# Attention and a feed-forward layer in one kernel: half of the small loads on GpSimd's queue, two pairs of token blocks merged, and a new written-out order

## The chip, the core and the metric

The kernel runs on one core of one Trainium2 chip. The metric is the device time of one execution in microseconds (us). The core has TensorE for matrix multiplication (PE in the profile; its weight loads are PEld), VectorE (DVE), ScalarE (ACT), GpSimd (POOL) and SyncE (SP), which here only issues transfers and transposes by DMA. Each engine works through its own instructions strictly in the order in which the program lists them.

## What is computed

The input is q, k and v for 4 batches, 12 heads, 448 tokens and 64 columns per head, all float32, and two weight matrices.

```python
scores = q @ k.T / sqrt(64)                    # causal: masked above the diagonal
attn = exp(scores - max) / (sum + 1e-9)
x = (attn @ v) as (4 * 448 tokens, 768)        # heads side by side
h = x @ w_in                                   # 768 -> 2048
g = h * sigmoid(1.702 * h)
out = g @ w_out                                # 2048 -> 768, (1792, 768) float32
```

## The kernel before

**Chunks and blocks.** The 1,792 tokens are 28 chunks of 64. `TUNE["groups"]` cuts them into nine blocks, each a run of chunks of one batch: block 0 is chunks 0 to 3 of batch 0, block 1 chunks 0 to 2 of batch 1, blocks 2 and 3 are chunks 0 to 3 and 4 to 6 of batch 2, blocks 4 and 5 the same of batch 3, blocks 6 and 7 chunks 3 to 4 and 5 to 6 of batch 1, and block 8 chunks 4 to 6 of batch 0. A block's width for TensorE is 64 columns for each of its chunks: 256, 192, 256, 192, 256, 192, 128, 128 and 192.

**Attention of a block** runs over six units u of two heads. Blocks 0 and 1 compute in float32 and turn q and k on TensorE (`load_heads`, `turn`, `k_unit32`, `q_unit32`; lines 888 to 953). From block 2 on, every float32 operand is split into two float16 parts, and k and q come in pairs of units: `k_pair` (from line 955) loads k for units u and u+1 with four transfers (line 965: units a = 0, 1, heads j = 0, 1 of each) into the one buffer `kk`, finds its scale, splits it and turns it with a DMA transpose (line 990); `q_pair` (from line 997) does the same for q with four transfers (line 1010) into the one buffer `qq`, copies each part once more (line 1053 on GpSimd or 1051 on VectorE), and `q_unit` turns it (line 1068). Then come the scores (1090 in float32, 1099 in float16), the mask and row maximum (1122), the exponential (1136), the row sums' small instructions (1256, 1262), the split of the probabilities, a DMA transpose of them (1283), and the product with v (1302), whose result for two units is written as two float16 parts into `xT`.

**The weights.** `w_in` and `w_out` come in as raw words and are put into another form by ScalarE and VectorE (`to_f32`, lines 541 to 592), summed for their scale (`gram`, line 616) and split in two float16 parts (`split`). A slice of `w_out` is loaded raw into a borrowed buffer that `TUNE["raw"]` names: W for the weights' own room, K for `kk`, V for `vraw`, P for the probabilities.

**The feed-forward layer of a block.** `moe(n)` calls `h_slice` for eight slices of 256 columns of w_in: 72 matmuls of the block's width for each slice (line 410, in four groups of 18; each instruction works on a 64-column half, and the two halves stand next to each other in the order), then tanh on ScalarE (1401) and the product on VectorE (1406), and the result is split into `gT`. `out_tile` (two chunks at a time) multiplies `gT` with w_out: 8 groups of 12 matmuls of 384 columns (line 1442) for each half of the output, one scaling instruction (468) and the store (1468). `xT` and `gT` are rings with places for seven chunks.

**The order.** Every step is registered with `add`: which engines could do it, what it reads and writes. The program is not emitted in the order of registration but in that of the string `ORDER`: a number is the step, the letter the engine (S for SP, P for TensorE, A, D, and G for GpSimd). The list before has 2,968 steps: 806 of TensorE, 1,033 of VectorE, 645 of ScalarE, 335 of SP and 149 of GpSimd. All transfers are S. The numbers in the braces of an `add` call are the planner's costs with which such an order was made; they put nothing into the program.

Of the kernel before, what the change touches and what calls it, by code (L numbers as in the profile page):

```python
# [9 lines left out]
F32 = mybir.dt.float32  # L10
# [16 lines left out]
    raw=(['W11', 'K0', 'V0', 'P0', 'W13', 'W15', 'K0', 'P0'], ['W11', 'W13', 'W15', 'V0', 'K0', 'P0', 'V0', 'P0']),  # L27
# [22 lines left out]
    wi2=2.63,  # L50
    parts=(((0, 1), (1, 3), (3, 6)), ((0, 3), (3, 6))),
# [3 lines left out]
1D 3G 2A 60S 0G 4S 45S 57S 9S 541G 14S 108S 61P 49S 5A 62A 6D 7A 84P 27S 8D 47S 58P 85A 59A 111S 10D 82P 491S 11A  # L55
46S 70P 12A 83D 13D 15A 159S 63P 71D 162S 73D 16A 109P 64D 447S 66D 74A 17D 93P 444S 72A 110D 65A 18D 86P 67A 75P
77D 96D 19P 28A 78D 94D 32S 87D 133P 89D 97A 20D 29D 79P 48S 95A 76D 21P 68P 88A 112P 22D 90A 30D 80A 98P 24D 100D
23D 113A 31D 134A 432S 121P 69A 101D 25A 99D 135P 122D 114P 124D 50S 91P 136D 123A 160P 115D 117D 125A 144P 26D 118A
436S 116A 137P 161A 163P 92A 102P 145D 164A 215S 147D 184P 146A 140D 210S 128D 148A 186P 138D 494S 129D 185D 141A
119P 103D 434S 172P 33A 187D 165P 139A 34D 81P 538S 173D 35A 168D 126P 166D 433S 175D 188P 169A 151D 120D 195P 167A  # L60
36D 174A 437S 51P 176A 191D 189D 152D 127A 196D 104P 198D 192A 52D 37P 190A 179D 228S 105D 197A 573S 53P 130P 216D
199A 545S 448P 54D 38D 217A 180D 202D 445P 56D 55D 131D 39P 149P 617D 40D 449D 106A 153P 218D 446A 42D 469P 107D
211A 142P 203D 450P 219D 150A 233S 467P 143A 435S 132P 212D 154A 470A 451D 155P 43A 213D 453D 170P 214D 177P 468A
457P 156D 452A 181P 251S 171A 41D 44D 178A 471P 193P 157A 200P 182A 454A 495P 458D 229A 204P 158D 246S 478P 194A
472D 492P 474D 459A 230D 183P 201A 479D 220P 205A 462D 231D 496A 493A 626D 324S 206P 463D 473A 232D 480A 497P 475A
504P 207D 552A 514P 221D 455P 500D 234A 498D 222P 483D 516P 505D 264S 484D 438P 223D 515A 456D 208A 235D 460P 225D
517A 439D 618P 236D 226A 209D 518P 336S 237D 440P 619P 461A 252A 224D 227D 238P 499A 501A 464P 247A 269S 525P 620P
253D 465A 635D 506A 521D 254D 476P 522A 248D 621P 553A 255D 477A 330S 325A 627P 239D 249D 622A 441D 481P 519D 250D
520A 240P 539P 482A 628P 265A 287S 443D 509D 526D 510D 241D 623D 527A 574P 629P 540A 266D 624A 243D 242D 530D 267D
244A 256P 282S 625D 630P 268D 575A 337A 485P 257D 245D 466P 631A 258P 576P 300S 487P 270A 636P 632D 486A 271A 259D  # L70
577D 502P 261D 644D 488D 637P 633A 544S 579D 272D 262A 593P 634D 638P 273D 503A 645P 288A 263D 305S 578A 639P 594A
489A 260D 274P 580A 289D 640A 531D 490D 507P 283A 646P 275D 641D 508A 290D 276P 331A 595P 284D 511P 291D 647P 301A
285D 642A 583P 277D 512A 302D 648P 596A 326A 286D 523P 643D 597P 649A 292P 279D 524A 303D 551A 654P 327D 280A 293D
304D 294P 528P 513P 295D 328D 306A 655P 297D 281D 529A 354S 298A 532P 534P 656P 307D 533A 550A 299D 581P 308A 657P
582A 338A 309D 318S 332A 278D 584D 310P 339D 585A 650D 604P 333A 311D 586P 340D 312P 651A 313D 598D 587A 588D 360S
600D 355A 315D 589D 535D 590P 652D 316A 653D 605D 663P 662D 334D 599A 601A 317D 393S 591A 319A 602P 658A 664P 320D
606A 342S 659D 603A 348S 536A 321D 607P 356A 665P 609D 296D 537D 777S 322D 660A 592P 361A 666P 661D 375S 608A 357D
362A 323P 610D 672P 671D 314D 358D 667A 611P 363D 394A 399S 673P 668D 612A 442D 680D 364D 613P 669A 674P 343A 670D
# [12 lines left out]
1031A 1346D 770G 709D 894S 772A 926D 733P 797D 1032D 928G 710D 864G 811A 746P 1193S 798A 927G 800A 773D 809A 734P
711A 1194S 812D 1039A 747P 799D 774S 712D 1033A 735P 1195A 801D 817D 713A 810D 748P 819D 845S 830D 930A 828D 736P
818A 714D 844S 932G 820A 829A 749P 842S 931D 821G 831A 843S 722D 715A 1034D 737P 933G 822D 1040D 1073S 1196A 832G
1052D 750P 716D 823A 1192S 825A 1200A 833D 824D 738P 826D 836A 1076S 1349D 1347D 1361D 751A 834D 837D 717A 881P 813S
835D 1053P 1362D 1041D 1199A 718D 846A 870P 1054P 1075S 882D 1202A 884D 739P 838S 719A 873D 871D 1042D 883A 906P
720D 885A 895P 847P 1055P 1074S 874A 848D 886G 872A 850D 849D 740P 959S 1201A 851D 929G 1198A 875G 887D 1056P 852D
1197A 741A 934S 814P 888A 876D 1203D 890D 1047A 753P 877D 889D 879A 891D 853S 1077A 1057P 907D 909D 908A 878D 754P
880D 910A 896D 1078D 898D 897A 911G 1058P 742S 1048D 899A 1080G 1079D 892S 1049A 1081D 900G 912D 755P 915A 913D
1050D 1082A 1204P 839P 901D 916D 904A 1209S 1084G 756P 914D 902A 1083D 840A 1208S 905D 1059P 1085G 903D 841D 1211S
757P 1205D 917S 1207D 1206G 946P 935P 1929D 758P 1994D 947D 938D 1086S 948A 936D 1060P 949D 939A 2540D 937A 950A  # L100
759P 1210S 940D 941D 951D 942A 944D 960P 752S 952D 971P 945D 953A 760P 943D 1132S 955A 963D 954D 964A 1108S 918P
961D 956D 761A 893P 972D 962A 1087P 974D 1063P 973A 965G 1995D 957S 975A 2553D 919A 1088P 966D 1061D 976G 1064P
# [102 lines left out]
class Ops:  # L205
# [16 lines left out]
    @staticmethod  # L222
    def turned(tiles):

        return {"SP": max(1.6, 0.2 * tiles - 0.65)}
# [66 lines left out]
def kernel(  # L292
# [74 lines left out]
    ps_o, ps_o_r = bufs(2, [P, 512], F32, "ps_o", pp)  # L367
    ps_t = ps_o[0]
    XC = 448
    ps_x_r = Ring(2)  # L370

    w_in32 = w_in.bitcast(I32)
    w_out32 = w_out.bitcast(I32)
# [1194 lines left out]
```

## Time and profile before

| | |
|---|---|
| median of 3 runs | 582.08 us (581.81 to 583.6) |
| the profiled execution's own time | 581.97 us |
| its span, first to last instruction | 580.3 us, 24,080 instructions |
| TensorE (PE) busy | 564.2 us, 97% of the span |
| its weight loads (PEld) busy | 475.5 us, 82% |
| VectorE busy | 424.6 us, 73% |
| ScalarE busy | 365.2 us, 63% |
| GpSimd busy | 60.8 us, 10% |
| granted TensorE clock | 1.000 over the whole span (full speed, 2.4 GHz) |
| chain that ended last | PE 78%, DVE 12%, DMA 4%, ACT 2%, issue 1% |

A span is the time from the first to the last instruction; what the execution's own time has over it lies before and after. Busy time is the union of an engine's instructions. A matmul's own duration is longer than the step from one matmul to the next, since they are pipelined; the steady cost of a group is read where the same group repeats without a gap.

### The profile page before, as it was taken

To read this page: it belongs to the slowest core of one execution; us is meant where nothing else is said; L and a number is where in the kernel's file an instruction comes from. 1 tells how busy PE (TensorE), PEld (TensorE's weight loads), DVE (VectorE), ACT (ScalarE), POOL (GpSimd) and SP (SyncE) were. 2 spreads that over 40 slices of the span, in tenths; PEclk is the share of its full clock that TensorE was granted. 3 is DMA by queue.
4 is the path that set the end of the run, shared out by engine and by line. 5 is a ranking of instruction groups with operands and counts; after the bars stand their busy time and mean duration, and the time that the engine had idled before them with its cause. 6 is when DMAs were issued, how large, how long until landed. Compare 5 with 4: busy or idle time off the path is not lost.

```text
span 580.3 us, 24080 instructions
## 1 busy us (share of the span) xinstructions
PE 564.2 (97%) x10376; PEld 475.5 (82%) x10376; DVE 424.6 (73%) x1201; ACT 365.2 (63%) x879; POOL 60.8 (10%) x165
## 2 busy tenths in 40 slices
PE   6999979999999999999999999999999999999997
PEld 4778868988788998779977899778987978889965
DVE  3899999999998688778758759555887987823110
ACT  5899999899976566458746556364665555512210
POOL 2000000013120102101100103011102020000000
PEclk9999999999999999999999999999999999999999
DMA  8999659588997968899846967877758957620010
GB/s 267 268 275 371 199 165 334 180 190 161 187 194 152 155 124 155 141 164 170 155 71 130 154 122 111 130 157 132 119 110 141 139 97 113 107 61 3 16 28 28
DMA packets 228187, 86.70 MB, mean 149 GB/s; under 512 B 208880, under 2 KB 217840, under 8 KB 228080
## 3 DMA queue, kind: packets, MB, share of 16 engines
q1 hardware_dynamic: 228080, 85.16, 72.4%
q8 instruction: 81, 1.33, 1.0%
q14 instruction: 26, 0.21, 0.1%
HBM read 44.63 MB, written 5.51 MB: 86 GB/s over the span
## 4 chain that ended last, share of the span: by engine, by line
PE 78%; DVE 12%; DMA 4%; ACT 2%; issue 1%; SPq 1%; DVEq 0%; ACTq 0%
PE ps_o L1442 33%; PE ps_h L410 30%; PE ps_v L1302 5%; PE ps_s L1099 5%; DVE wob L592 2%; DVE wob L473 2%; PE ps_s L1090 2%; PE ps_o L913 2%; DMA wob<-in_moe_w_out_dram 2%; DMA gT<-in_k_dram 1%; PE ps_h L903 1%; DVE ps_h L1406 1%; DVE wob L558 1%; DMA out_dram<-ob 1%; DVE wob L577 1%
## 5 line engine op out<-in xcount | busy, mean ns | idle before, releaser
L410 PE MATMUL ps_h<-xT,wib 128*64 128x192 f16 (+2 forms) x5184 | 247.7, 249 | 1.2 <-DVE gT L473 0.9
L1442 PE MATMUL ps_o<-wob,gT 128*64 128x384 f16 x2688 | 237.3, 326 | 0.5 <-DVE wob L473 0.5
L410 PEld LDWEIGHTS <-wib 128*64 128x64 f16 x5184 | 224.9, 110 | 10.9 <-issue 3.2
L1442 PEld LDWEIGHTS <-gT 128*64 128x64 f16 x2688 | 153.2, 110 | 54.4 <-issue 0.9
L1136 ACT ACTIVATE z<-z,cols 128x384 f32<-128x384 f32 (+6 forms) x140 | 72.8, 521 | 56.3 <-DVE cols L1122 48.3
L1122 DVE CUSTOM_DVE_ANT_0 z<-ps_s,mask,cols 128x384 f32<-128x384 f32 (+6 forms) x126 | 62.6, 519 | 26.4 <-PE ps_s L1099 25.4
L1401 ACT ACTIVATE t<-ps_h,cols 128x384 f32<-128x384 f32 (+2 forms) x72 | 42.3, 587 | 45.8 <-PE ps_h L410 44.0
L473 DVE SCALAR_TENSOR_TENSOR p<-z,cols,p 128x384 f16<-128x384 f32 (+3 forms) x126 | 67.6, 558 | 3.4 <-ACT p L468 2.7
L1406 DVE SCALAR_TENSOR_TENSOR ps_h<-t,ps_h 128x384 f32<-128x384 f32 (+2 forms) x72 | 41.3, 574 | 37.4 <-ACT t L1401 37.0
L468 ACT ACTIVATE p<-z,cols 128x384 f16<-128x384 f32 (+3 forms) x78 | 41.7, 555 | 9.5 <-DVE cols L1262 4.9
L1099 PE MATMUL ps_s<-kT,qT 128*64 128x384 f16 (+5 forms) x504 | 45.5, 288 | 0.3 <-DMA kT<-kk 0.3
L473 DVE SCALAR_TENSOR_TENSOR gT<-ps_h,gT 128x384 f16<-128x384 f32 (+2 forms) x72 | 40.9, 567 | 6.5 <-ACT gT L468 6.3
L1302 PE MATMUL ps_v<-PT,v 128*64 128x192 f16 (+7 forms) x924 | 42.7, 237 | 0.0
L468 ACT ACTIVATE gT<-ps_h 128x384 f16<-128x384 f32 (+2 forms) x60 | 30.1, 501 | 18.1 <-DVE ps_h L1406 17.2
L468 ACT ACTIVATE ob<-ps_o,cols 128x384 f32<-128x384 f32 x24 | 13.9, 577 | 38.1 <-PE ps_o L1442 35.4
L1302 PEld LDWEIGHTS <-v 128*64 128x64 f16 x828 | 32.8, 110 | 2.1
L1256 POOL TENSOR_SCALAR cols<-cols 128x2 f32<-128x2 f32 (+1 forms) x53 | 14.4, 272 | 158.3 <-ACT z L1136 157.7
L1099 PEld LDWEIGHTS <-qT 128*64 128x64 f16 x504 | 24.5, 110 | 4.7 <-issue 0.4
L1053 POOL TENSOR_SCALAR qq<-qq 128x384 f16<-128x384 f16 (+2 forms) x32 | 20.9, 655 | 54.6 <-ACT qq L468 32.4
L1136 ACT ACTIVATION_READ_ACCUMULATOR z<-z,cols 128x1 f32 x140 | 26.5, 189 | 0.0
L449 POOL TENSOR_SCALAR cols<-cols 128x1 int32<-128x1 int32 x18 | 8.5, 470 | 164.2 <-DVE cols L435 163.9
L470 DVE TENSOR_SCALAR p<-z,cols 128x384 f16<-128x384 f32 (+3 forms) x48 | 22.8, 487 | 1.0
(121 smaller groups left out, 598.5 us busy)
## 6 DMA issues: line engine op xcount, KB each, us to landing
wob<-in_moe_w_in_dram SPq DMA_DIRECT2D x15, 768.0 KB, 7.4
kk<-in_k_dram SPq DMA_DIRECT2D x48, 112.0 KB, 3.3
vraw<-in_v_dram SPq DMA_DIRECT2D x12, 384.0 KB, 5.7
wob<-in_moe_w_out_dram SPq DMA_DIRECT2D x6, 768.0 KB, 6.5
out_dram<-ob SPq DMA_DIRECT2D x22, 192.0 KB, 2.4
p<-in_moe_w_out_dram SPq DMA_DIRECT2D x4, 768.0 KB, 7.1
kk<-in_moe_w_out_dram SPq DMA_DIRECT2D x3, 768.0 KB, 7.9
vraw<-in_moe_w_out_dram SPq DMA_DIRECT2D x3, 768.0 KB, 4.9
```

The source lines that it names most:

```text
L410: nc.tensor.matmul(out[o : o + 64], lhsT[:, o : o + 64], rhs, start=start, stop=stop)
L468: nc.scalar.activation(out=dst, in_=src, func=AF.Copy, scale=sc)
L470: nc.vector.tensor_scalar(out=dst, in0=src, scalar1=sc, scalar2=None, op0=ALU.mult)
L473: nc.vector.scalar_tensor_tensor(out=dst, in0=src, scalar=sc, in1=hi, op0=ALU.mult, op1=ALU.subtract)
L1053: nc.gpsimd.tensor_scalar(out=dst, in0=src, scalar1=1.0, scalar2=1.0, op0=ALU.mult, op1=ALU.mult)
L1099: nc.tensor.matmul(ps[64 * j : 64 * j + 64], qt[:, g, i - c0, 64 * j : 64 * j + 64], kt[:, : i + 1, 64 * j : 64 * j + 64], start=(g == 0), ...
L1122: lambda e: nc.vector.tensor_tensor_reduce(out=z[:, :w], in0=ps, in1=mask[:, S - w :], scale=c, scalar=3.0e38, op0=ALU.add, op1=ALU.min, a ...
L1136: lambda e: nc.scalar.activation(out=z[:, :w], in_=z[:, :w], func=AF.Exp, bias=m, scale=-1.0, accum_out=l),
L1302: nc.tensor.matmul(ps[64 * j : 64 * j + 64, 64 * (first - c0) : w], vt[:, J, j] if f32(gr) else vt[:, gv, J, j, :], (p_f32(pi)[:, at] if f ...
L1401: lambda e: nc.scalar.activation(out=th, in_=ph, func=AF.Tanh, scale=ts[:, sl : sl + 1]),
L1406: lambda e: nc.vector.scalar_tensor_tensor(out=ph, in0=th, scalar=1.0, in1=ph, op0=ALU.add, op1=ALU.mult),
L1442: nc.tensor.matmul(po[64 * j : 64 * j + 64, :OH], gT[:, r, gg, f], wo_pair(f, gw, nh), start=(f == 0 and gg + gw == 0), stop=(f == NFC - 1 ...
```

## The change

1. **Queues.** In `k_pair` and `q_pair` the two transfers of the second unit (a = 1) are issued from GpSimd instead of SP: 24 transfers of k and 42 of q. Sizes, sources and targets are the same.
2. **Wider blocks.** `TUNE["hb"]` merges blocks 4 and 5, and blocks 6 and 7, for the first half of the feed-forward layer. Blocks 4 and 5 become one of seven chunks, 448 columns wide; since two times 448 columns do not fit a 512-column PSUM bank, each slice is done as two parts of 128 columns of w_in, each with its own tanh, product and split. Blocks 6 and 7 become one of four chunks, 256 columns wide. 224 matmul groups of TensorE remain for the output; those of `h_slice` go from 288 to 224.
3. **Raw buffers.** Two slices of w_out that were loaded into `kk` go to V and W15 instead; one stays in `kk`.
4. **Small steps.** The largest scale of w_in is taken once (`w_in_largest`) instead of once for each half of the output.
5. **Order.** A new `ORDER` with 2,870 steps: 742 of TensorE, 1,010 of VectorE, 635 of ScalarE, 269 of SP and 214 of GpSimd. Step numbers up to 317 mean the same in both lists; from 430 to 1926 a step of the new list is the one with a number higher by two in the old.
6. The other edits change the planner's costs (the numbers in the braces), or add switches that are off (`gram_p`, `vg`, `pt`, `zs`) or at their old meaning (`og`, `ig`, `ko`).

```diff
-    raw=(['W11', 'K0', 'V0', 'P0', 'W13', 'W15', 'K0', 'P0'], ['W11', 'W13', 'W15', 'V0', 'K0', 'P0', 'V0', 'P0']),
+    raw=(['W11', 'K0', 'V0', 'P0', 'W13', 'W15', 'V0', 'P0'], ['W11', 'W13', 'W15', 'V0', 'W15', 'P0', 'V0', 'P0']),
...
+    hb=((0,), (1,), (2,), (3,), (4, 5), (6, 7), (8,)),
...
 ORDER = """
-1D 3G 2A 60S 0G 4S 45S 57S 9S 541G 14S 108S 61P 49S 5A 62A 6D 7A 84P 27S 8D 47S 58P 85A 59A 111S 10D 82P 491S 11A
-46S 70P 12A 83D 13D 15A 159S 63P 71D 162S 73D 16A 109P 64D 447S 66D 74A 17D 93P 444S 72A 110D 65A 18D 86P 67A 75P
...
+1D 3G 2A 4S 0G 57S 60S 9S 14S 45S 539G 5A 27S 6A 442S 58P 7A 108S 8D 111S 61P 59A 47S 82P 62A 10D 162S 11A 63P 445S
+83D 12A 84P 66D 64D 67A 13D 70P 15A 159S 85D 86P 65A 46S 73D 16A 68P 71D 87D 93P 89D 69D 88A 17D 90A 72A 28D 91P 74A
...
+362S 316A 584P 330D 661P 596D 533D 656A 558S 560G 317D 662P 357A 559G 557S 597A 585A 663P 534A 657D 350S 321A 586D
...
+    parts_of = {ns[0]: ns for ns in TUNE["hb"]}
+    wide = {n: sum(blocks[x][2] - blocks[x][1] for x in ns) for n, ns in parts_of.items()}
...
         for a in range(2):
             for j in range(2):
                 keys += [("kf", a, j)]
                 add(
-                    {"SP": 0.78},
-                    lambda e, a=a, j=j: nc.sync.dma_start(
+                    {"POOL": 0.75} if a else {"SP": 0.78},
+                    lambda e, a=a, j=j: (nc.gpsimd if e == "POOL" else nc.sync).dma_start(
                         out=kf[64 * j : 64 * j + 64, a], in_=k[b, 2 * (u + a) + j].rearrange("(c p) d -> p c d", p=64)
...
-                    {"SP": 0.81},
-                    lambda e, a=a, j=j: nc.sync.dma_start(
+                    {"POOL": 0.75} if a else {"SP": 0.81},
+                    lambda e, a=a, j=j: (nc.gpsimd if e == "POOL" else nc.sync).dma_start(
                         out=f[64 * j : 64 * j + 64, a * ni : (a + 1) * ni],
...
     def h_slice(n, sl, prio):
-        _, c0, c1, gr = blocks[n]
-        w = 64 * (c1 - c0)
+        gr = blocks[n][3]
+        nc_ = wide[n]
+        w = 64 * nc_
         r = first_at[n] % GT
+        nt = 2 if 2 * w <= 512 else 1
+        for t0 in range(0, 2, nt):
+            h_part(n, sl, t0, nt, nc_, w, r, gr, prio + t0 / 2)
+
+    def h_part(n, sl, t0, nt, cn, w, r, gr, prio):
         hb = sl % 2 if n == 0 else ps_h_r.next()
-        ph = ps_h[hb][:, : 2 * w]
+        ph = ps_h[hb][:, : nt * w]
...
-        if n:
-            moe(n - 1)
-    moe(NB - 1)
+        for x in range(n + 1):
+            if x in parts_of and x not in done and (parts_of[x][-1] < n or wide[x] > 4 or n == NB - 1) and parts_of[x][-1] <= n:
+                done.append(x)
+                moe(x)
```

In the lists, 4S, 9S and 14S load parts of w_in's first slice, 57S and 60S the heads of k and q for the first two units, 45S v; 58P and 61P turn k and q of unit 0, 82P and 84P those of unit 1, and 63P and 70P are the first scores. In the new list 557S, 558S, 559G and 560G are the first load of k for block 2 (559 to 562 in the old).

## Rows read from the trace of the kernel before

**Rows 1.** Stretches of core 0: us, then busy time (instructions) of each engine, clock, DMA.

```profile
core 0: us, PE busy (x) PEld busy (x) DVE busy (x) ACT busy (x) POOL busy (x), PEclk, DMA share, GB/s
0.00:20.00 20.00, 14.80 (x152) 9.97 (x154) 10.23 (x39) 12.73 (x33) 3.09 (x19) 1.00 0.95 257
...
80.00:140.00 60.00, 54.10 (x1184) 49.42 (x1182) 58.94 (x134) 55.99 (x93) 4.54 (x11) 1.00 0.80 218
140.00:200.00 60.00, 58.95 (x888) 49.76 (x885) 52.03 (x171) 45.05 (x130) 12.72 (x30) 1.00 1.02 176
200.00:560.00 360.00, 360.00 (x6886) 306.61 (x6882) 245.73 (x685) 191.80 (x479) 40.41 (x105) 1.00 0.68 115
...
sum 581.00, PE 564.24 PEld 475.46 DVE 424.59 ACT 365.17 POOL 60.75; mean PE 94.04 PEld 79.24 DVE 70.76 ACT 60.86 POOL 10.13
```

**Rows 2.** TensorE in order of time, the first instruction and the last.

```profile
3.82 1.12 PE L913 MATMUL ps_o<-ident,gT 128*64 128x128 f32 x8 [3.82 <-DMA gT<-in_q_dram]
...
571.76 5.04 PE L1442 MATMUL ps_o<-wob,gT 128*64 128x384 f16 x60
```

**Rows 3.** What TensorE waited for: us in total, times, longest.

```profile
PE ps_h L1201 <- ACT PT L468: 1.1, 1, 1.1
...
PE ps_s L1099 <- DMA kT<-kk: 0.3, 1, 0.3
PE ps_s L414 <- ACT kk L458: 0.2, 1, 0.2
```

**Rows 4.** The chain that ended last, in order of time: runs of one width without a gap.

```profile
191.19 8.84 PE ps_h L410 x162
...
268.33 5.20 PE ps_h L410 x126
...
458.60 4.02 PE ps_h L410 x144
...
550.48 26.34 PE ps_o L1442 x324
```

**Rows 5.** The start, in order of time: SP's issues, TensorE's first turn of k, first scores.

```profile
0.79 0.45 SPq L894 DMA_DIRECT2D gT<-in_q_dram  x1
...
1.30 0.49 SPq L650 DMA_DIRECT2D wob<-in_moe_w_in_dram  x1
1.83 0.43 SPq L829 DMA_DIRECT2D v<-in_v_dram  x1
...
2.31 0.51 SPq L894 DMA_DIRECT2D gT<-in_k_dram  x1
...
6.48 0.72 PEld L913 LDWEIGHTS ps_o<-ident,gT 128*64 128x64 f32 x8 [0.36 <-DMA gT<-in_k_dram]
...
9.42 2.40 PE L1090 MATMUL ps_s<-kT,qT 64*64 64x192 f32 x16
```

**Rows 6.** DMA: GB/s in 40 slices of the span, and one issue with its size.

```profile
GB/s 267 268 275 371 199 165 334 180 190 161 187 194 152 155 124 155 141 164 170 155 71 130 154 122 111 130 157 132 119 110 141 139 97 113 107 61 3 16 28 28
...
v<-in_v_dram SPq DMA_DIRECT2D x12, 128.0 KB, 6.3
```

**Rows 7.** Instructions on k and q by line: ns shortest/median/longest, first and last start.

```profile
L965 SPq DMA_DIRECT2D kk<-in_k_dram x48: 596/628/1749, 115.2 to 432.5; - x48
...
L473 DVE SCALAR_TENSOR_TENSOR kk<-kk,cols x12: 1136/1148/1152, 126.0 to 443.3; 128x896 f16<-128x896 f32 x12
...
L470 DVE TENSOR_SCALAR kk<-kk,cols x5: 682/687/698, 160.2 to 426.4; 128x896 f16<-128x896 f32 x5
...
L1010 SPq DMA_DIRECT2D qq<-in_q_dram x84: 595/610/2072, 88.9 to 462.2; - x84
```

**Rows 8.** GpSimd's small scale instruction: ns shortest/median/longest.

```profile
L449 POOL TENSOR_SCALAR cols<-cols x18: 190/191/1286, 118.6 to 467.9; 128x1 int32<-128x1 int32 x18
```

**Rows 9.** What ScalarE waited for at the loads of q and k.

```profile
ACT waste L458 <- DMA qq<-in_q_dram: 3.7, 4, 1.4
...
ACT kk L458 <- DMA kk<-in_k_dram: 2.4, 1, 2.4
```

More of the change, by code (lines that the diff above doesn't have):

```diff
@@ L223, in turned @@
     def turned(tiles):
[L225 removed]
+        return {"SP": max(1.55 + 0.04 * tiles, 0.33 * tiles - 2.45)}
     @staticmethod
@@ L423, in all_sum @@
         else:
-            row, key = ps_o[1][:, :1], ("O", 1)
+            row, key = turn[0][:, :1], turn[1]
         half = src.bitcast(BF16)[:, 1:2]
@@ L619, in mm @@
                     )
-        add({"PE": len(blocks) * 0.0585}, mm, [k for _, keys in parts for k in keys], ps_keys, prio)
+        add({"PE": len(blocks) * 0.036}, mm, [k for _, keys in parts for k in keys], ps_keys, prio)
     def gram_max(ps, ps_key, sq, sq_key, prio, n=64):
@@ L794, in v_batch @@
         sq, sq_key = col("sqv1", 2)
+        if g in TUNE["vg"]:
+            x = ps_x_r.next()
+            ps = ps_s[x][:, XC:]
+            gram_of([(vraw.rearrange("p j h d -> p j (h d)"), [("vraw", j, h) for j in range(NJ) for h in range(2)])], ps, [("X", x)], prio)
+            gram_max(ps, ("X", x), sq, sq_key, prio)
+            v_scale(g, sq, sq_key, "X", prio)
+            return
         for j in range(2 * NJ):
@@ L1268, in unit @@
         if f32(gr):
+            if n in TUNE["pt"]:
+                p_turned(n, range(c0, c1), zx, pi, where, prio)
+        if f32(gr) and n not in TUNE["zs"]:
             la, ra = la[:, c0:c1], ra[:, c0:c1]
@@ L1321, in unit @@
         sc_keys = [bst[gr]["s_v_key"]] * ap
-        if f32(gr):
+        if f32(gr) and n not in TUNE["zs"]:
             add(
@@ L1390, in h_slice @@
                     mm,
-                    [("wi", sl, 0), ("wi", sl, 1)] + [("xT", r + x, u, g) for u in range(a, a + half) for g in range(2) for x in range(c1 - c0)],
+                    [("wi", sl, 0), ("wi", sl, 1)] + [("xT", r + x, u, g) for u in range(a, a + half) for g in range(2) for x in range(cn)],
                     [("H", hb)], 1e6 + prio + t / 2,
@@ L1411, in h_slice @@
         gain = 2.0**-25
[L1412 to L1416 removed]
+        f0 = 2 * sl + t0
+        hi, lo = (gT[:, r : r + cn, g, f0 : f0 + nt].rearrange("p r f t -> p r (f t)") for g in range(2))
+        full = ph.rearrange("p (r x) -> p r x", x=64 * nt)
+        keys = [[("gT", r + a, f, g) for a in range(cn) for f in range(f0, f0 + nt)] for g in range(2)]
+        add({**act(nt * w, psum=True), **dve(nt * w)}, lambda e: scaled(e, hi, full, gain), [("H", hb)], keys[0], p0)
+        add(dve(nt * w), lambda e: rest(lo, full, gain, hi), [("H", hb)] + keys[0], keys[1], p0)
     def out_tile(tt, prio):
@@ L1475, in moe @@
     def moe(n):
-        _, c0, c1, gr = blocks[n]
+        gr = blocks[n][3]
         for s in range(NWS):
@@ L1486, in moe @@
                 out_scale(gr, nh, n * 100 + 30 - 1e6)
-        for i, tt in enumerate(range(first_at[n] // 2, (first_at[n] + c1 - c0) // 2)):
+        for i, tt in enumerate(range(first_at[n] // 2, (first_at[n] + wide[n]) // 2)):
             out_tile(tt, n * 100 + 40 + i)
```

519 lines of the change are left out of this document (278 added, 241 removed).

## The prediction

> **What bounds the kernel now.** I began with the busy table by stretch [rows 1]. From 200 to 560 us TensorE is busy 360.00 of 360.00 us at the full granted clock, while VectorE has 245.73 and ScalarE 191.80: in this stage nothing that those two engines or the queues do is on the path, and only TensorE's own work counts. Before it the picture is another one. From 80 to 140 us TensorE idles 60 - 54.10 = 5.9 us, with VectorE busy 58.94 and ScalarE 55.99 of 60: here the conversion of the weights and the float32 attention fill both, and TensorE waits for them. In the first 20 us it idles 5.2 us, from 140 to 200 us 1.05 us.
>
> The whole idle time of TensorE is 580.3 - 564.24 = 16.1 us. Its first matmul starts at 3.82 us, on the first load, and its last ends at 571.76 + 5.04 = 576.8 us, after which come one scaling and one store [rows 2]. So 3.8 us of head and 3.5 us of tail are fixed for this change, and 8.8 us lie between. The view of waits [rows 3] shows them in small pieces behind ScalarE's and VectorE's results, the longest 1.1 us; two of them, 0.3 + 0.2 = 0.5 us, name the keys of block 2.
>
> So the change can gain in three ways only: less TensorE work, an earlier start of the work on the two full engines, or less idle time before 200 us. More speed of the queues after 200 us gains nothing; there, the change can only lose, if a late load makes TensorE wait.
>
> **The wider blocks.** They cost fewer matmuls for the same columns. The steady step comes from runs without a gap [rows 4]: 8.84 us / 162 = 54.6 ns for 256 columns, 5.20 / 126 = 41.3 ns for 192, 4.02 / 144 = 27.9 ns for 128. From 128 to 256 columns the step grows by 26.7 ns, 0.208 ns a column, which leaves about 1.2 ns that do not depend on the width. The 384-column products fit: 26.34 / 324 = 81.3 ns, against 1.2 + 80.1. For 448 columns I therefore take 1.2 + 93.4 = 94.6 ns. A block has 8 x 72 = 576 such instructions, so blocks 4 and 5 go from 576 x (54.6 + 41.3) = 55.2 us to 576 x 94.6 = 54.5 us, and blocks 6 and 7 from 576 x 2 x 27.9 = 32.1 us to 576 x 54.6 = 31.4 us. Together -1.4 us. This lies in the stage where TensorE never idles, so it counts in full. The bounds are 0 (the wide form has some fixed cost of its own) and -2.0 (the fixed part being 1.7 ns).
>
> The seven-chunk block also takes away freedom. Its first product needs all seven places of the rings `xT` and `gT`: the outputs of blocks 2 and 3 must have been read out of `gT` before it fills them, and block 6 cannot write `xT` before it has ended, 54.5 us of TensorE's work later. I cost that at nothing: what hides it is the 48 output groups of tiles 7 to 9, which become ready as that product ends, 48 x 12 x 81.3 ns = 47 us. If that cover were gone, the loss would be the chain from the last wide group to block 6's next products; it stays in the case of no change below.
>
> **The start.** The first scores need q and k of block 0. Today q's heads are the first issue at 0.79 us and k's the fourth at 2.31 us, behind q, a part of w_in and v; TensorE's first turn of k loads at 6.48 us, after a wait that names that load, and the first scores start at 9.42 us [rows 5]. In the new list w_in's part is first, k second, q third, v behind the rest of w_in. What has to land for the scores is smaller by v's 128 KB, which at the 267 GB/s of that slice is 0.5 us [rows 6]; and of the four turns of heads that stand ahead of the scores today one, unit 1's of q, is moved behind them. A turn is 1.12 us [rows 2]; since most of this one runs while k is still awaited, I count half, 0.5 us. w_in's first part is issued at 0.79 instead of 1.30 us, 0.5 us sooner. All work of the two full engines begins with these two. I take -1.0 us. The bounds are 0 (q, now third, is what the scores wait for) and -1.4 us, all that TensorE idles in the first 20 us beyond the 3.8 us of the first load.
>
> **The stage to 200 us.** The list has the same conversions and attention in another order, so VectorE's and ScalarE's sums do not shrink and I expect most of the idle to stay. Two raw slices less in `kk` let block 2's first k load go out ahead of the second half of w_out, where it is issued at 115.2 us now [rows 7]; that can take away the two waits that name it, -0.5 us. The bounds are the 5.9 + 1.05 = 7.0 us of idle on the one side and, on the other, the same size as the longest wait today, +1.1 us, for a new one.
>
> **The loads on GpSimd.** 66 issues leave SP, 42 of q at 0.61 us and 24 of k at 0.63 us [rows 7]: 41 us of SP's time, all off the path, since TensorE waits for none of it after 200 us. They enter GpSimd's list, between the small instructions of the scales (449), the row sums (1256) and the copies of q (1053). Behind an issue that waits for `kk` or `qq` to be free these wait too, and for them ScalarE's splits, the transposes on SP and at last the scores. No row shows GpSimd issuing a transfer. Below, I bound one at 0.2 us (the usual 190 ns of its smallest instruction); above, by the longest time that this instruction took, 1.29 us [rows 8]. I take the price of SP's issue, 0.6 us, since it is the same transfer: 40 us more on an engine that has 40.41 of 360 us busy, at no cost to the end. What hides it is how early the loads go out: of 33 groups of loads (21 of q, 12 of k) ScalarE was idle until one landed only five times (3.7 us for q in 4 cases, 2.4 us for k in one [rows 9]), and no wait of TensorE came of it.
>
> The stretched instruction itself is the place where a rule bears on this. On VectorE the one-input split of k takes 687 ns and the two-input rest of the same 896 elements 1148 ns [rows 7], so the first runs in a faster mode; and GpSimd's scale of one column took 190 ns in the median and 1,286 ns once. The Trainium skill (SBUF — State Buffer, section "SBUF: two separate sides") says that for a transfer issued from GpSimd the descriptors are written by GpSimd's own cores, and that VectorE in a mode that uses both ports locks them out for its whole instruction, so that the transfer starts late. By that page the loads would come late wherever VectorE splits at that time; no run here has shown it yet, and it is the first rival.
>
> **Sum.** 581.97 (the profiled execution) - 1.4 - 1.0 - 0.5 = 579.1 us; the median stands 0.1 us above the profiled execution, so 579.2 us.
>
> **Rivals.**
> *GpSimd's issues are slow (slower).* Each pair of loads takes 2 x (1.29 - 0.61) = 1.4 us longer than on SP, and holds up the small instructions behind it. The five loads that ScalarE already waited for have nothing to spare; if each stops TensorE, whose order is fixed, the loss is 5 x 1.4 = 7.0 us: 586.2 us. It decides from the third late pair on, since two cost 2.8 of the 2.9 us gained. For it speaks that the new list leaves TensorE more after the last product with v, 60 groups of output instead of 35 (25 x 12 x 81.3 ns = 24 us), so attention has to run 24 us faster and has less to spare. Against it: the SP queue loses 41 us of issues, and the full stage shows no TensorE wait at all. Chance 0.20.
> *Nothing measurable (same).* The merge gives its 1.4 us or part of it, and the start and the middle stay, because q is now the late load and VectorE sets the pace: 580.7 us at the full 1.4, 582.1 at none. Chance 0.25.
> *The new order closes the gaps before 200 us.* With all 8.8 us gone and the merge, 581.97 - 10.2 = 571.8 us; with half of them, 576.2 us. For it: these are many small waits, which an order can move. Against it: VectorE has 1.06 us left of 60 there. Chance 0.15.
>
> **How the numbers follow.** A change within 0.3% (1.7 us: below 580.3 or above 583.8) is about what a measurement of this kernel can't tell from none. The forecast of 579.2 us, with a range of its own from 577.0 to 580.3, has 0.40. Faster is then 0.40 + 0.15 = 0.55, same 0.25, slower 0.20. For 8 in 10 I leave out the end of the closed gaps below 575 us and slow issues that stop TensorE more than five times, above 586.2 us.
>
> **What would show it.** Right: 4,032 instructions in the first product at about 94.5 ns for 448 columns; first scores before 8.5 us; TensorE without idle from 200 us on; idle between head and tail near 7 us. Wrong: TensorE waiting, after 140 us, for scores or products with v behind q's or k's loads or behind GpSimd; GpSimd's small instructions much longer than 190 ns in the median; or a gap between the wide product and block 6.

## The result, and the profile after

The changed kernel is slower: 588.66 us in the median of 8 runs (586.16 to 591.24) against 582.53 us for the kernel before on the same chip (581.63 to 584.79, 8 runs). The ratio is 1.0096, with a 95% interval of 1.0069 to 1.0123. The profiled execution took 586.17 us, its span is 584.2 us, and the granted clock is 1.000 over it. It is nearly the shortest of the eight, so its trace explains about 4 of the 6.1 us.

The first view is the busy table by stretch of the changed kernel; columns as in [rows 1].

```profile
0.00:20.00 20.00, 13.61 (x150) 9.41 (x150) 9.84 (x38) 12.40 (x34) 3.09 (x19) 1.00 0.99 261
20.00:80.00 60.00, 58.04 (x1034) 45.56 (x1032) 58.08 (x179) 55.83 (x140) 0.00 (x0) 1.00 0.82 247
80.00:140.00 60.00, 54.26 (x1187) 49.89 (x1184) 56.26 (x129) 51.78 (x92) 12.75 (x20) 1.00 0.90 230
140.00:200.00 60.00, 57.14 (x853) 48.31 (x850) 54.94 (x179) 48.59 (x134) 20.10 (x44) 1.00 0.97 171
200.00:560.00 360.00, 359.51 (x5770) 316.55 (x5768) 237.17 (x658) 195.39 (x470) 68.66 (x148) 1.00 0.66 116
```

TensorE's idle time, 60 or 20 or 360 minus its busy time, against [rows 1] and the one row of the kernel before that is not there:

```profile
20.00:80.00 60.00, 59.59 (x1086) 48.19 (x1084) 57.66 (x176) 57.28 (x143) 0.00 (x0) 1.00 0.86 261
```

| stretch | before | after |
|---|---|---|
| 0 to 20 us | 5.20 | 6.39 |
| 20 to 80 us | 0.41 | 1.96 |
| 80 to 140 us | 5.90 | 5.74 |
| 140 to 200 us | 1.05 | 2.86 |
| 200 to 560 us | 0.00 | 0.49 |
| whole span | 16.1 | 21.1 |

So 5.0 us of idle time came in, 1.1 us of work went out (TensorE is busy 563.1 us, 564.2 before), and 5.0 - 1.1 = 3.9 us is what the span grew. VectorE, which was full from 80 to 140 us, now has 56.26 us there instead of 58.94: it, too, is kept waiting, and its work is done later.

The row from 80 to 140 us hides two changes that nearly cancel. Cut into pieces, first the kernel before, then the changed one:

```profile
80.00:108.00 28.00, 23.48 (x515) 21.39 (x513) 27.24 (x69) 26.34 (x44) 0.00 (x0) 1.00 0.90 291
108.00:120.00 12.00, 11.61 (x301) 11.04 (x298) 12.00 (x20) 11.03 (x17) 0.34 (x2) 1.00 0.48 117
```

```profile
80.00:108.00 28.00, 26.38 (x570) 24.37 (x567) 27.53 (x63) 27.56 (x48) 4.82 (x6) 1.00 1.04 309
108.00:120.00 12.00, 8.16 (x195) 7.42 (x192) 8.77 (x21) 8.02 (x12) 1.25 (x2) 1.00 1.09 212
```

Up to 108 us the new order closes gaps, and TensorE's idle time falls from 4.52 to 1.62 us; in the 12 us behind, it rises from 0.39 to 3.84 us.

What TensorE waited for (answers [rows 3]; us in total, times, longest), and then the longer of these waits in order of time, the wait in brackets; between the first two, every row:

```profile
PE ps_o L929 <- DMA gT<-in_k_dram: 5.0, 1, 5.0
PE ps_o L625 <- issue: 3.8, 2, 2.6
PE ps_h L419 <- DVE gT L482: 2.4, 4, 1.0
PE ps_s L1115 <- DVE cols L1138: 1.3, 1, 1.3
PE ps_s L423 <- DVE cols L819: 1.0, 1, 1.0
```

```profile
111.03 0.26 PE L625 MATMUL ps_o<-wob 128*64 128x64 bf16 x4 [2.57 <-issue]
111.12 3.88 PE L419 MATMUL ps_h<-xT,wib 128*64 128x192 f16 x90
114.84 1.14 PE L1496 MATMUL ps_o<-wob,gT 128*64 128x384 f16 x12
115.81 0.91 PE L419 MATMUL ps_h<-xT,wib 128*64 128x192 f16 x18
116.56 0.23 PE L625 MATMUL ps_o<-wob 128*64 128x64 bf16 x4
118.05 0.32 PE L625 MATMUL ps_o<-wob 128*64 128x64 bf16 x8 [1.27 <-issue]
172.85 0.19 PE L423 MATMUL ps_s<-cols 128*64 128x1 bf16 x2 [0.95 <-DVE cols L819]
182.68 0.52 PE L1115 MATMUL ps_s<-kT,qT 128*64 128x384 f16 x4 [1.28 <-DVE cols L1138]
```

Two groups stand out, 108 to 118 us and 172 to 183 us. The two waits of the first group (2.57 + 1.27 = 3.84 us) have no named releaser, and each stands in the middle of a group of twelve sums of w_out. From the one to the other TensorE does 4 + 90 + 12 + 18 + 4 = 128 matmuls; with a weight load for each, that is 256 instructions. The pages of the two kernels list a queue that brings instructions (packets, MB, share of the span), first before, then after:

```profile
q8 instruction: 81, 1.33, 1.0%
```

```profile
q8 instruction: 72, 1.18, 0.8%
```

Each packet has 16,384 bytes. TensorE has 2 x 10,376 instructions before and 2 x 9,224 after, which is 81.1 and 72.1 times 256: each packet is a block of 256 of its own instructions, and both waits stand where one block ends and the next begins. In the packet records of the changed kernel, TensorE begins a block at 103.95 us, the packet of the next block starts only at 108.32 and ends at 109.44 us, and TensorE goes on at 111.03; the packet behind the second wait ends at 116.82 us, and TensorE goes on at 118.05. In the kernel before, TensorE begins the same block at 103.65 us, the next one's packet starts at 106.20, and the wait is 0.21 us. So in these two waits TensorE waits for its own program.

What the queue was doing then, SP and ScalarE show: SP's issues from 99 us on (start, duration), then ScalarE's square of k.

```profile
99.60 1.79 SPq L719 DMA_DIRECT2D wob<-in_moe_w_out_dram  x2
101.44 1.34 SPq L1026 DMA_DIRECT2D qq<-in_q_dram  x1
103.33 4.76 SPq L1006 DMA_TRANSPOSE kT<-kk  x1
108.15 1.71 SPq L981 DMA_DIRECT2D kk<-in_k_dram  x2
109.97 0.56 SPq L719 DMA_DIRECT2D vraw<-in_moe_w_out_dram  x1
```

```profile
116.60 0.95 ACT L467 ACTIVATE kk<-kk 128x896 bf16<-128x896 f32 x1 [3.98 <-DMA kk<-in_k_dram]
```

The new order sends out block 2's first k early, as the prediction said, and so its transpose and the four loads of the second pair go out between the slices of w_out. The transpose holds SP for 4.76 us; the second pair's loads leave at 103.7 us (GpSimd) and 108.15 us (SP), need 7.8 to 9.9 us to land, and ScalarE, whose list has the square of that k next, stands for 3.98 us. VectorE then waits 3.04 us for ScalarE; no wait of TensorE names either of them here. The DMA view of 95 to 120 us shows how full the queue is, first of the kernel before, then of the changed one (the queue's packets, MB and share; then issues with KB and median us to landing):

```profile
q1 hardware_dynamic: 4356, 5.39, 69.3%
wob<-in_moe_w_out_dram SPq DMA_DIRECT2D x2, 768.0 KB, 6.5
kk<-in_k_dram SPq DMA_DIRECT2D x4, 112.0 KB, 2.7
```

```profile
q1 hardware_dynamic: 5242, 6.42, 98.1%
q0 software_dynamic: 160, 0.36, 9.7%
kk<-in_k_dram POOLq DMA_DIRECT2D x2, 112.0 KB, 9.9
kk<-in_k_dram SPq DMA_DIRECT2D x2, 112.0 KB, 7.8
kT<-kk SPq DMA_TRANSPOSE x1, 11.8
```

The same 112 KB landed in 2.7 us before, where they leave at 115 us behind most of w_out, and in 7.8 to 9.9 us now.

### The profile page after: what moved, and what is told of

The parts are those of the page before. It is cut to its first block, busy times and chain, and to the rows that moved or that the text cites. A ratio compares the mean times of both kernels' runs of the same rounds, so it can differ in the third digit from the quotient of the medians.

```text
span 584.2 us, 21799 instructions
## 1 busy us (share of the span) xinstructions
PE 563.1 (96%) x9224; PEld 487.2 (83%) x9224; DVE 416.3 (71%) x1178; ACT 366.3 (63%) x869; POOL 104.6 (18%) x230
## 4 chain that ended last, share of the span: by engine, by line
PE 78%; DVE 11%; DMA 5%; ACT 3%; issue 2%; SPq 1%; DVEq 0%; ACTq 0%
PE ps_o L1496 32%; PE ps_h L419 31%; PE ps_s L1115 5%; PE ps_v L1344 5%; PE ps_o L929 2%; PE ps_s L1106 2%; DVE wob L601 2%; DMA kk<-in_k_dram 1%; DVE wib L482 1%; DVE wob L586 1%; DMA vraw<-in_v_dram 1%; DVE z L1138 1%; DMA qT<-qq 1%; DMA PT<-p 1%; ACT z L1152 1%
## 5 line engine op out<-in xcount | busy, mean ns | idle before, releaser
L419 PE MATMUL ps_h<-xT,wib 128*64 128x256 f16 (+2 forms) x4032 | 242.2, 273 | 2.5 <-DVE gT L482 2.4
L419 PEld LDWEIGHTS <-wib 128*64 128x64 f16 x4032 | 207.9, 110 | 20.6 <-issue 4.4
L1496 PEld LDWEIGHTS <-gT 128*64 128x64 f16 x2688 | 177.0, 110 | 32.6
L1455 DVE SCALAR_TENSOR_TENSOR ps_h<-t,ps_h 128x512 f32<-128x512 f32 (+2 forms) x64 | 40.1, 627 | 68.7 <-ACT t L1450 68.3
L1450 ACT ACTIVATE t<-ps_h,cols 128x512 f32<-128x512 f32 (+2 forms) x64 | 40.4, 632 | 57.0 <-PE ps_h L419 56.9
L477 ACT ACTIVATE p<-z,cols 128x512 f16<-128x512 f32 (+3 forms) x81 | 44.1, 564 | 17.9 <-DVE cols L1301 13.0
L482 DVE SCALAR_TENSOR_TENSOR gT<-ps_h,gT 128x512 f16<-128x512 f32 (+2 forms) x64 | 39.6, 620 | 8.9 <-ACT gT L477 8.6
L477 ACT ACTIVATE gT<-ps_h 128x512 f16<-128x512 f32 (+2 forms) x52 | 28.2, 542 | 18.5 <-DVE ps_h L1455 18.3
L981 POOL DMA_DIRECT2D kk<-in_k_dram x24 | 17.7, 740 | 109.0 <-DVE ps_v L1367 82.5
L1026 POOL DMA_DIRECT2D qq<-in_q_dram x42 | 26.7, 638 | 17.3 <-issue 8.7
```

The lines of the kernel that those rows point to most:

```text
L419: nc.tensor.matmul(out[o : o + 64], lhsT[:, o : o + 64], rhs, start=start, stop=stop)
L477: nc.scalar.activation(out=dst, in_=src, func=AF.Copy, scale=sc)
L482: nc.vector.scalar_tensor_tensor(out=dst, in0=src, scalar=sc, in1=hi, op0=ALU.mult, op1=ALU.subtract)
L1026: lambda e, a=a, j=j: (nc.gpsimd if e == "POOL" else nc.sync).dma_start(out=f[64 * j : 64 * j + 64, a * ni : (a + 1) * ni], in_=q[b, 2 * ( ...
L1450: lambda e: nc.scalar.activation(out=th, in_=ph, func=AF.Tanh, scale=ts[:, sl : sl + 1]),
L1455: lambda e: nc.vector.scalar_tensor_tensor(out=ph, in0=th, scalar=1.0, in1=ph, op0=ALU.add, op1=ALU.mult),
```

## The experiments

Theory A, formed from this: the new order puts k's and v's transfers among those of w_out and their first use close behind, so that engines wait for landings before 200 us. Theory B: GpSimd's issues are slow. Theory C: the seven-chunk block costs more than it saves. Rivals D and E came up later and stand in the expectations; so does the "rival C" of the run with later checks, which is another one.

**The queues.** One run puts all 66 loads back on SP in the changed kernel, one puts them on GpSimd in the kernel before; in both, order and places are kept.

```diff
-                    {"POOL": 0.75} if a else {"SP": 0.78},
+                    {"SP": 0.78},
...
-                    {"SP": 0.78},
+                    {"POOL": 0.75} if a else {"SP": 0.78},
```

> The changed kernel with all 66 loads back on SP, at the same places of the same order. Theory A (the new order: loads of k and v for blocks 2 and 3 stand among the raw loads of w_out, and ScalarE, which works in order, waits for them): the time stays at that of the changed kernel within 1.5 us, 586 to 590 us, with the 3.8 us wait near 108 to 118 us still there. Theory B (GpSimd's issues are slow or block its small instructions): it falls back to 582 us or below. Should SP's queue be what the loads were moved away from, it grows by some us instead.

> The kernel before with only the loads of the second unit on GpSimd, at the same places of its own order. Theory A: 581.5 to 583.5 us, no TensorE idle after 200 us. Theory B: slower by 3 us or more, 585 us and above, with waits behind the loads of k and q.

All on SP: 597.71 us, ratio 1.0243 (1.0222 to 1.0264), some us more, as the last sentence of the expectation allowed. TensorE then idles 6.4 us even after 200 us, so the new order needs the second queue. The kernel before with GpSimd's loads: 582.07 us, 0.9976 (0.9957 to 0.9995). Theory B falls: in the order of before these loads cost nothing and may gain a little.

**The merge.** The blocks are taken apart again, in the places of the merged ones (30 steps had to move).

```diff
-    hb=((0,), (1,), (2,), (3,), (4, 5), (6, 7), (8,)),
+    hb=((0,), (1,), (2,), (3,), (4,), (5,), (6,), (7,), (8,)),
+    when={4: 5, 5: 5, 6: 8, 7: 8},
...
```

> The changed kernel with blocks 4 and 5, and 6 and 7, as separate blocks again, in the places that the merged ones have in the new order (30 steps had to move a little). Theory A: slower than the changed kernel by the 1.4 us of the extra instructions, 587.5 to 591 us. Theory C (the seven-chunk block costs more than it saves): faster than the changed kernel, 585 us or less.

597.58 us, 1.0255 (1.0200 to 1.0309), 6 us above what theory A had at most. TensorE waits 10.9 us for `gT` in the narrow groups, since that order was made for wide ones; so this run says little of the merge itself, except that TensorE is busy 3.4 us more.

**The start.** Steps 4S (w_in) and 57S (k) change places.

```diff
-1D 3G 2A 4S 0G 57S 60S
+1D 3G 2A 57S 0G 4S 60S
```

> The changed kernel with the first two issues exchanged: the heads of k go out before w_in's first part. TensorE starts near 3.8 us instead of 5.0. Theory A: 0.5 to 1.2 us faster than the changed kernel if the start is on the path, and no difference if VectorE's and ScalarE's conversions, which now start later, set the pace.

588.02 us, 1.0084 (1.0054 to 1.0114). TensorE starts at 4.0 us instead of 5.04 and still idles 6.4 us of the first 20: the first load alone is not what sets the time. Whether the start as a whole does, this run can't tell, since the idle time there stayed.

**Old and new order spliced.** In the changed kernel's code the first part of the list comes from the old order (its steps renumbered, the loads of a = 1 on GpSimd), then follow the steps of the new list that are still missing; or the reverse. One thing goes with it: where the old order covers the second half of w_out's loads (the cuts at 118, 155, 175 and 195 us, and the old order from 80 to 155 us), w_out's raw buffers are the old ones too.

```diff
-    raw=(['W11', 'K0', 'V0', 'P0', 'W13', 'W15', 'V0', 'P0'], ['W11', 'W13', 'W15', 'V0', 'W15', 'P0', 'V0', 'P0']),
+    raw=(['W11', 'K0', 'V0', 'P0', 'W13', 'W15', 'K0', 'P0'], ['W11', 'W13', 'W15', 'V0', 'K0', 'P0', 'V0', 'P0']),
...
```

> The changed kernel's code (merged blocks, loads of the second unit on GpSimd) with the old list's steps in their old order up to about 175 us, after that the new list; the raw buffers of w_out are the old ones. Theory A (the new order loses its time before about 175 us, where weights, the first attention and the first loads of k share the transfers): TensorE idles as before up to 175 us (about 12 us), the merge's 1.3 us remain, so 580 to 581 us. Rival D (the time goes after 175 us, in the merged blocks and what is packed around them): 586 us or more, as the changed kernel.

> The same, but the old order only up to about 118 us, where the last raw slice of w_out has been loaded. If the whole loss of Theory A lies in the first 118 us (start behind w_in, waits up to 80 us, the load of k at 108 to 116 us): 580 to 581 us as with the later cut. If the batch of v at 165 to 172 us and what follows it costs as well: 582.5 to 584 us. Rival D: 586 us or more.

> The reverse: the kernel before (blocks not merged) with GpSimd's loads and the new raw buffers, in the new order up to about 175 us and the old one after. Theory A: the loss is there without the merge, and the merge's 1.3 us are missing: 587 to 590 us. Rival D: 582 to 583 us, since the part to blame is not in it.

> The changed kernel's code with the old list's order up to about 195 us, after all four loads of block 4's first keys and the batch of v, and the new list after. The cut at 175 us stood in the middle of these loads: it took the load of k late, as the old list has it, and ScalarE's square of it early, as the new one has it, and ScalarE waited 5.85 us for it. If the merged stage itself is sound (Theory A): before's idle time up to 195 us (about 13 us), the merge's 1.1 to 1.4 us gained: 580 to 581.5 us. If the loss lies in the merged stage (rival D): 585 us or more.

> The same with the old order up to about 155 us. Against the cut at 195 us it tells what the new order's places for k and v of batch 3 at 155 to 195 us cost. Theory A, from the idle time of the two traces between 140 and 200 us (1.05 us before, 2.86 after): 2 us more than the cut at 195, 582 to 583.5 us. If these places cost nothing: the same as that cut.

> The old order up to about 80 us, then the new list with the eight later steps of the run with later checks (585.98 us). TensorE's idle time in the first 80 us is 5.6 us before and 8.4 us after, so Theory A expects 2.8 us less than that run: 582.5 to 584 us. If the conversions after 80 us set the time and early waits of TensorE are absorbed there, no gain: 585.5 to 586.5 us.

> The changed kernel's code and order, with the old order only between about 80 and 155 us. If the loss of the new order is made in that stretch (weights of the second product, first keys of block 2, transposes), and the 2.8 us more idle time of TensorE in the first 80 us are absorbed where VectorE is full: 581 to 582.5 us, as with the old order from the start to 155 us (581.44). If the start costs its idle time: 584 to 585 us.

> The same with the new order up to about 118 us and the old one only from there to 155 us. If the loss lies in the stretch of 99 to 116 us, where two slices of w_out, a transpose of k and four loads of k stand one behind the other: 585 to 588 us, as the changed kernel. If it lies behind it (first scores of block 2 asked for too early): 581 to 583 us.

| order | us | ratio, interval | longest new waits (of TensorE, where not said) |
|---|---|---|---|
| old to 175 us, then new | 586.62 | 1.0077 (1.0051 to 1.0104) | 4.15; ScalarE 5.85 for k |
| old to 118, then new | 589.32 | 1.0110 (1.0076 to 1.0143) | 3.00 for k's transpose |
| new to 175, then old, not merged | 588.92 | 1.0108 (1.0085 to 1.0131) | 1.89 for `gT`; 2.27 for a transpose of the probabilities |
| old to 195, then new | 588.85 | 1.0102 (1.0080 to 1.0123) | 5.92 for q's transpose |
| old to 155, then new | 581.44 | 0.9984 (0.9967 to 1.0001) | none over 1.0 |
| old to 80, then later checks | 588.10 | 1.0086 (1.0061 to 1.0112) | 2.46 for `gT` |
| new, old from 80 to 155, new | 588.91 | 1.0104 (1.0079 to 1.0128) | 6.81; ScalarE 6.30 for w_out |
| new, old from 118 to 155, new | 595.90 | 1.0218 (1.0191 to 1.0246) | 7.41; ScalarE 6.03 for v |

The new order without the merge is as slow as the changed kernel, but by waits that are in part its own, and its trace has none at the ends of TensorE's blocks; so it says little against rival D. The cut at 155 us, meant to be slower than that at 195, settles that: the new order behind 155 us, with both merged blocks, runs as fast as before. What costs the time is therefore the new order before 155 us together with its raw buffers, which these runs don't separate. The busy table of that run, from 80 us on, has TensorE idle 2.7, 1.1, 0.7, 0.7 and 0 us:

```profile
80.00:115.00 35.00, 32.32 (x708) 29.58 (x708) 34.93 (x81) 33.31 (x54) 2.42 (x4) 0.95 0.78 257
115.00:140.00 25.00, 23.93 (x494) 21.55 (x491) 24.11 (x52) 23.29 (x47) 9.90 (x18) 1.00 0.93 181
140.00:175.00 35.00, 34.26 (x486) 27.58 (x481) 33.36 (x114) 29.50 (x86) 14.43 (x30) 1.00 1.23 186
175.00:200.00 25.00, 24.30 (x396) 22.80 (x397) 22.29 (x72) 16.06 (x46) 6.89 (x17) 1.00 0.97 172
200.00:230.00 30.00, 30.00 (x565) 29.23 (x562) 29.41 (x69) 23.96 (x52) 10.34 (x21) 1.00 1.04 166
```

Most of the others missed their numbers for a reason that is itself a finding: at the seam one list issues a transfer late and the other uses it early, and TensorE waits 3 to 7 us for one such step. They can't split the stretch before 155 us any further.

**Steps moved inside the new order.** First the square of k's second pair (765A) goes 39 places later, and the last two squares of v with v's sum and scale (1199A to 1205D) about 45 places. Then, on top, k's transpose (568S), the second pair's loads and the square move behind w_out's last slices.

```diff
-992D 996P 719D 1049D 689D 765A 721P
+992D 996P 719D 1049D 689D 721P
...
-614D 568S 763G 355P
+614D 355P
```

> The changed kernel with eight steps of its order moved: ScalarE's square of k's second pair of block 2 goes behind seven more of ScalarE's other steps, and the last two squares of v's batch 3 with its sum and scale 45 steps later. Theory A: the waits of 4.0 us (ScalarE for k) and 0.95 us (TensorE for v's sum) go and TensorE gets 3 to 4.5 us of them back: 584 to 586 us. Rival C (VectorE and ScalarE are full there, so a removed wait comes back as another): 587.5 to 589 us.

> The run with later checks (585.98 us) with six steps more moved: the transpose of k's first pair goes behind the last slice of w_out, and the four loads of k's second pair and its square follow 20 to 30 steps later, so that none of them is between the loads of w_out. Theory A: k's loads land in about 4 us instead of 8 to 10, the waits of 2.5 and 0.4 us that TensorE has in the sums of w_out go, and 2 to 3 us are gained: 583 to 584.5 us. If those waits have nothing to do with these transfers: 585.5 to 587 us.

Later checks: 585.98 us (582.98 to 590.98, 11 runs), 1.0075 (1.0046 to 1.0103). The median is 2.7 us below that of the changed kernel, inside what theory A had, but the two intervals overlap, so a gain is not shown. In its trace ScalarE no longer waits for that k, yet TensorE still waits 2.51 us at the same end of a block: ScalarE's wait was not what held TensorE there. The second: 588.82 us (584.55 to 593.04), 1.0106 (1.0063 to 1.0149), not what was expected. Its waits in the sums of w_out did shrink (0.45 and 1.41 us), but now q's loads are late: ScalarE waits 5.13 us for one at 136 us, and TensorE 3.09 us right after. The wait moved on to the next transfer, and the two runs don't tell theory A from the rival that a removed wait comes back as another.

**The disputed cost by itself.** The order is left alone, and the transfers of w_out's second half are cut from 768 to 32 KB, in the changed kernel and in the one before. Both leave out most of the weights of the output's second half, and only their time is read.

```diff
-                out=flat.bitcast(I32).rearrange("p (a n) -> p a n", a=2), in_=src
+                out=flat.bitcast(I32).rearrange("p (a n) -> p a n", a=2)[:, : 2 - nh, : (64 if nh else 2 * OH)],
+                in_=src[:, : 2 - nh, : (64 if nh else 2 * OH)],
```

> The changed kernel with the eight transfers of w_out's second half cut from 768 KB to 32 KB each (128 rows of 64 words; the rest of the buffer holds what was there, so the second half of the output is wrong and only the time is read). All steps, queues and waits stay. Theory A (transfers of k and v land late behind those of w_out, and the steps that the new order has put close behind them wait): the waits of 4.0 us for k, of 2.6 and 1.3 us in the sums of w_out go, 4 to 6 us are gained: 583 to 585 us, and most of the distance to the kernel before closes when both are run so. Rival E (it is the order of the engines' own steps, whatever the transfers do): under 1.5 us is gained: 587 to 588.7 us.

> The control: the same cut in the kernel before. By both theories little is gained, since its longest wait is 1.1 us and none of that length names a transfer: 581 to 582.5 us. Theory A: the distance from the changed kernel with the same cut is 2.5 us or less; rival E: 5 us or more.

Changed kernel: 582.90 us, 0.9996 (0.9980 to 1.0012). Kernel before: 580.98 us, 0.9980 (0.9962 to 0.9997). The cut gives the changed kernel 588.66 - 582.90 = 5.8 us and the one before 582.76 (its median beside these runs) - 580.98 = 1.8 us, and the distance between them falls from 6.1 to 1.9 us (the ratios, each against the kernel before on the same chip, say the same); by the two intervals, the 1.9 is good to about 1.4 us. Rival E falls. The DMA view of 95 to 120 us, three rows of the busy table and ScalarE's square of k, of the changed kernel so cut:

```profile
q1 hardware_dynamic: 4476, 1.52, 38.6%
kk<-in_k_dram POOLq DMA_DIRECT2D x2, 112.0 KB, 6.4
kk<-in_k_dram SPq DMA_DIRECT2D x2, 112.0 KB, 5.5
```

```profile
80.00:108.00 28.00, 25.33 (x531) 23.14 (x528) 26.16 (x60) 26.20 (x46) 4.80 (x6) 1.00 0.74 175
108.00:120.00 12.00, 11.73 (x280) 10.87 (x276) 11.93 (x26) 11.51 (x17) 1.25 (x2) 1.00 0.45 85
120.00:140.00 20.00, 19.89 (x426) 17.72 (x424) 19.97 (x52) 16.08 (x38) 9.20 (x12) 1.00 0.48 108
```

```profile
114.81 0.95 ACT L467 ACTIVATE kk<-kk 128x896 bf16<-128x896 f32 x1 [0.49 <-DMA kk<-in_k_dram]
```

From 108 to 120 us TensorE idles 0.27 us instead of 3.84, and from 80 to 140 us 2.67 + 0.27 + 0.11 = 3.05 us instead of 5.74. Both waits at the ends of TensorE's blocks are gone: the next block's packet now starts at 105.40 us, before TensorE crosses into the block ahead of it at 105.66. ScalarE's wait for k falls from 3.98 to 0.49 us, though k still takes 5.5 to 6.4 us to land. That w_out's own slices land sooner is not what helps: in the changed kernel, neither ScalarE nor VectorE has a wait from 80 to 140 us that names one. This trace is of the longest of the twelve executions (587.17 us), which idles 4.38 us from 140 to 200 us, so it stands for this stretch and not for the median.

## Why the prediction was wrong, step by step

- **The wider blocks** (-1.4 us): right. A run of 72 instructions of 448 columns takes 6.84 us, 95.0 ns each against the 94.6 taken; TensorE's work fell by 1.1 us. The chain of waits, and the form among TensorE's groups:

```profile
390.52 6.84 PE ps_h L419 x72
```

```profile
L419 PE MATMUL ps_h<-xT,wib 128*64 128x448 f16 x576 | 57.6, 352 | 0.0
```

- **The lost freedom of the seven-chunk block** (0): right. With the cut at 155 us TensorE has no idle time from 200 to 560 us; the changed kernel has 0.49 us, at a transpose of the probabilities.
- **The loads on GpSimd** (0.6 us each, no cost): right. GpSimd spends 638 ns on an issue for q and 740 on one for k, and k lands 3.7 us after GpSimd's issue and 3.3 us after SP's (medians):

```profile
L1026 POOL DMA_DIRECT2D qq<-in_q_dram x42 | 26.7, 638 | 17.3 <-issue 8.7 <-DVE qq L1067 5.7 <-DVE cols L1295 1.2
L981 POOL DMA_DIRECT2D kk<-in_k_dram x24 | 17.7, 740 | 109.0 <-DVE ps_v L1367 82.5 <-DVE kk L482 21.2 <-DVE p L482 4.7
```

  So the first rival, whose 586.2 us lies next to the profiled 586.17, was near by chance: its mechanism is refuted by the 0.9976, and no TensorE wait of that kind is in the trace. The rule of the Trainium skill (SBUF — State Buffer, section "SBUF: two separate sides") is not contradicted, but no lateness from it shows in these medians.
- **The start** (-1.0 us): wrong. The first scores came at 9.09 us instead of 9.42, 0.33 us sooner, not 1.0; k, now the second issue, lands at 4.9 us and lets TensorE start at 5.04 us instead of 3.82. Idle time in the first 20 us rose by 1.2 us. The swap of the two issues moved the median by only 0.6 us, inside its interval, but left the idle time of these 20 us as it was; what the term itself is worth stays open.
- **The stage to 200 us** (-0.5 us, at worst +1.1): this is the step that failed. It was read that k's first load would go out ahead of w_out's second half, and only the waits it could take away were counted; those two did go. What goes with that load, its transpose and the next pair's four loads, was put at nothing in the queue, without a reason, and so was what a full queue does to the other transfers, TensorE's own program among them. And the bound for a new wait, the longest wait of before, was no bound: TensorE's new waits are 2.57 and 1.27 us for blocks of its program, then 1.28 and 0.95; ScalarE's is 3.98. The trace of before had the warning: 69% of the queue's time taken from 95 to 120 us, and 768 KB landing in 6.5 us.
- **The third rival**, the order closing these gaps, was right up to 108 us, where 2.9 us of them went, and wrong for the whole: 3.45 us came back in the 12 us behind, 1.8 us from 140 to 200 us, and 1.55 us from 20 to 80 us, there in small waits for VectorE and ScalarE, the longest 0.83 us.

Shown: GpSimd's queue and the merged stage are not to blame, the loss is made before 155 us, and 5.8 - 1.8 = 4.0 of its 6.1 us hang on the size of w_out's transfers. In the one trace, the waits that go with that size are the 3.84 us for TensorE's program. Open: how the 4.0 us divide between these blocks and the late k; and how much of the other 1.9 us belongs to the start, since the two splices that bear on it made waits of their own.

## What to carry to other kernels

A written-out order is a set of bets on when transfers land. Before pricing a new one, list for the stretch it changes every transfer with its size and time to landing, add those that move in, transposes too, and compare each landing with the place of its first use on an engine that can't look past it. TensorE's program is such a transfer too: here a block of 16 KB for every 128 matmuls with their weight loads. A bound for a new wait is the time to landing under that load, not the longest wait in the old trace.

## What the runs showed of the hardware

The waits at the ends of TensorE's blocks vary from run to run. At the same two ends they were 2.57 and 1.27 us in the changed kernel, 2.51 and 0.44 with the later checks, 0.65 and 0.17 with the swapped first issues, and in the kernel before 0.21 us at the first; the end before the first and the first took 0.51 and 1.08 us in the kernel before with GpSimd's loads. Neither run with thin transfers has one over 0.1 us. In the traces with such a wait of 0.4 us or more before 120 us, TensorE went on 1.2 to 1.9 us after the packet's end.

One wait was followed by a second loss in some runs. With the later checks, in the rows below, TensorE stood from 108 to 110.6 us, then the granted clock fell to 0.50 (1.2 of 2.4 GHz) from 112 to 114 us, and ScalarE waited 4.07 us for the slowed matmuls; in the changed kernel's profile the wait of 2.57 us at the same place had no fall behind it.

```profile
108.00:110.00 2.00, 0.14 (x10) 0.03 (x2) 2.00 (x5) 1.71 (x4) 0.00 (x0) 1.00 1.35 61
110.00:112.00 2.00, 1.35 (x26) 1.36 (x28) 2.00 (x5) 2.00 (x3) 0.00 (x0) 0.80 1.14 173
112.00:114.00 2.00, 2.00 (x30) 2.00 (x28) 2.00 (x6) 0.30 (x1) 1.34 (x2) 0.50 1.23 222
```

Of the eleven executions of that kernel the three with a mean clock of 1.000 took 582.98 to 585.16 us and the five with 0.993 or 0.994 took 587.45 to 590.98 us. The changed kernel's eight go the same way: 586.17 us at 1.000, 590.21 at 0.994 and 591.24 at 0.993. That falls of the clock behind such waits are what spreads them is likely, but no trace here shows a long execution of that kernel. The kernel before has no such spread: of the 23 executions beside the thin transfers, the six at 0.993 or 0.994 took 582.06 to 584.37 us and the seven at 1.000 took 581.09 to 585.63.
